# Nystrom attention into a sticky mixture of experts, one core: landmarks and C's row sums at other chunks, the first G in three pieces, and three smaller moves

## The chip, the cores and the metric

The kernel runs on one core of one Trainium2 chip. The metric is the device time of a run in microseconds (us), as the median of several runs. Engines are PE (matrix multiply), PEld (its weight loads), DVE (vector), ACT (scalar), POOL (GpSimd) and SP (the queue that issues most DMAs).

## The reference

```
# per batch b of 8; 8 heads, 576 tokens, 64 columns a head, 32 landmarks (means of 18 tokens)
A, Bm, C = sm(q, k_lm), sm(q_lm, k_lm), sm(q_lm, k)        # row softmaxes; C is 32 x 576
Z = Bm.T / (norm1(Bm) * norminf(Bm) + 1e-6)
for _ in range(6): Z = 2*Z - Z @ Bm @ Z
x = A @ Z @ C @ v                                          # 576 x 512 after joining the heads
logits = x @ w_gate;  local = sigmoid(x @ w_local)
# token s takes the expert of the token before it, unless s == 0 or local < 0.5: then argmax(logits)
p = softmax(logits)[e];  out[b, s] = p * (relu(x @ w1[e]) @ w2[e])     # 8 experts, 512 -> 1024 -> 512
```

## The kernel before

**What is computed where.** x is never formed. At, the transposed A (for all heads, 256 rows by 576 tokens), is split into a high and a low part (`ath`, `atl`); with W = Z C v, G = W w1[e] is formed once per batch in `w_w1` (L798: PE makes `pg` and `ph`; L804: ACT copies them rounded to `gh`; L807: DVE writes the rest, `gl`). `mm1` (L832) multiplies gh by ath, gh by atl and gl by ath into `ph`; ACT takes the relu (`h`, L839), DVE its low part (L844, and L847 for the last 64 tokens). The second product (L874, L883) multiplies h by `wh` and `wl`, the split of w2 (L819 on ACT, L821 on POOL), into `py` and `pg`. Each batch runs whole with the expert that most of its tokens chose; the other tokens go into 128 slots, which are done as a ninth, short pass.

**Order.** All of this is one stream written out by hand. An expert's pass over a batch is 16 chunks (`CH`), about 3.4 us each; `tick` advances a clock between chunks, and `at_time(t, fn)` queues a step that starts at chunk t and may `yield` a number of chunks before its next part. The attention of batch b is put in with `attention(b)`: each step has an offset in chunks to t0 = 16 (b - 1), from the table STEADY, or FIRST and SECOND for the batches 1 and 2. So the attention of a batch runs in pieces beside the expert passes of the one to three batches before it. In this text batch n is the stretch in which the expert's pass of batch n runs; batch 0 begins near 41 us, batch 1 near 106, and from there each takes 54.1 us; the slots' pass runs from about 466. A phase is a chunk within a batch. Every engine runs its instructions in program order and waits where one isn't ready.

**The steps that the change touches.** `load` brings q and k of a batch (two DMAs of 1152 KB on SP), `load_v` v. `landmarks` is called four times a batch (k, q, k, q): two adds on POOL (L200) into `t9`, of which there is one buffer, and a chunk later a reduce on DVE (L202), then ACT's scale (L210, L212). `c_sums` (L312 to L314) makes the reciprocal row sums of C, used by L299 in `c_v`. `gates` and `fresh` (L459 to L481) make the gate logits' maximum and the flag d (L478) that PE transposes at L490; `newton_start` (L358, L359) makes `et` for PE's L367. `own_rest` (L526 to L538) ends with a chain on a tile `psum`. `load_w1` and `load_w2` (L783, L812) bring the experts' weights as `raw`. `store` ends a block of 128 tokens; the last, half block adds two parts on POOL (L912) after ACT has read it (L909, L910). `others` finds the slots in batch 7: it sets tables with POOL memsets (L920, L921, L938) that a DVE scan reads (L927). `slot_tokens` makes one-hot rows on DVE (L1013) and gathers with them on PE (L1017); from the result come indices by which POOL fetches rows (L1040).

Of the kernel before, what the change touches and what calls it, by code (L numbers as in the profile page):

```python
# [12 lines left out]
F32 = mybir.dt.float32  # L13
# [4 lines left out]
ALU = mybir.AluOpType  # L18
# [42 lines left out]
def nystrom_attn_then_sticky_moe(ctx, tc, qT, kT, v, wg, w12, out):  # L61
    nc = tc.nc
# [70 lines left out]
    sm = ctx.enter_context(tc.tile_pool(name="sm", bufs=2))  # L133
# [24 lines left out]
    def at_time(t, fn, *args):  # L158
        heapq.heappush(events, (t, next(serial), fn, args))
# [12 lines left out]
    def at_once(parts):  # L172
        for _ in parts:
            pass
# [115 lines left out]
        nc.scalar.copy(out=st["ect"][0:rows, k0:k0 + nb, :], in_=pt[0:rows, 0:nb, :])  # L290

    def c_v(st):
        rs = c_sums(st)
        pv = one.tile([P, 2, D])
        for g in range(2):
            c_v_rows(st, pv, g, range(NBLK))
        yield 0.25
        st["u"] = sm.tile([P, 2, D], F32, name="u")
        nc.vector.tensor_tensor(out=st["u"], in0=pv, in1=rs.unsqueeze(2).broadcast_to([P, 2, D]), op=ALU.mult)  # L299
# [8 lines left out]
                                 st["v"][0:rows, k, D * h:D * h + D], start=(k == 0), stop=(k == NBLK - 1))  # L308

    def c_sums(st):  # L310
        rs = sm.tile([P, 2], F32, name="rsc")
        nc.vector.reduce_sum(out=rs, in_=st["sc"], axis=AX.X)  # L312
        nc.vector.tensor_scalar_add(rs, rs, 1e-9)
        nc.vector.reciprocal(out=rs, in_=rs)  # L314
        return rs
# [226 lines left out]
    def keep_busy(n):  # L542

        pz = one.tile([P, 512]).rearrange("p (a b) -> p a b", b=P)
        for _ in range(n):
            nc.tensor.matmul(pz, identb, ones.unsqueeze(1).broadcast_to([P, 4, P]), start=True, stop=True)

    def startup(st, nx):
# [77 lines left out]
        rs = sm.tile([P, 2], F32, name="rsb")  # L626
# [33 lines left out]
        rsc = c_sums(st)  # L660
# [15 lines left out]
        full = st["full"] = at.tile([P, 2, S], F32, name="at")  # L676
# [69 lines left out]
        own(0, st)  # L746

        e = st["e"] = expert_of(regs[0:1, 0:1])
        st["w1", 0] = load_w1(e, 0, 2)
        get_w2(0, 0)  # L750
        get_w2(0, 1)
        st["w1", 1] = load_w1(e, 1)
# [4 lines left out]
        lk0(2)  # L757
        c0 = scores_c(nx, 0)
        next(c0)
        keep_busy(5)  # L760
        lq2(4)
        rest = own_rest(0, st)
        next(rest)
        next(c0)
        nc.vector.tensor_tensor(out=al, in0=full, in1=ah.bitcast(F32), op=ALU.subtract)
        lk2(2)
        g0 = w_w1(st, 0, 0, 2)
        at_once(c0)
        next(g0)
        at_once(g0)  # L770
        at_once(rest)
        at_time(0.3, lk2, 2)

    behind = []

# [1 line left out]
        return nc.values_load(reg, engines=[ET.SP], min_val=0, max_val=E - 1,  # L777
                              skip_runtime_bounds_check_because="an expert")

    def load_w1(e, hf, nf=4):  # L780
        t = fw.tile([P, 4, 512], F32, name="raw1", bufs=2)
        for f in range(0, 4, nf):
            nc.sync.dma_start(out=t[:, f:f + nf], in_=w12[bass.ds(e, 1), 4 * hf + f:4 * hf + f + nf, :, 0:512].rearrange(  # L783
                "a f p x -> p (a f) x"))
        return t
# [111 lines left out]
    def store(b, st, k, yp):  # L897
        t0 = b * S + k * P
        if k < 4:
            ys = fk.tile([P, DM], F32, name="ys", bufs=2)  # L900
            nc.scalar.mul(out=ys, in_=yp, mul=st["pw"][:, k:k + 1])  # L901
            yield 0.5
            nc.sync.dma_start(out=out[t0:t0 + P, :], in_=ys)
        else:
            p = st["pw"][0:64, k:k + 1]
            yield 1.25
            ys = fk.tile([P, DM], F32, name="ys", bufs=2)
            yl = fk.tile([P, DM], F32, name="yl", bufs=1)
            nc.scalar.mul(out=ys[0:64], in_=yp[64:128], mul=p)  # L909
            nc.scalar.mul(out=yl[0:64], in_=yp[0:64], mul=p)  # L910
            yield 0.5
            nc.gpsimd.tensor_tensor(out=ys[0:64], in0=ys[0:64], in1=yl[0:64], op=ALU.add)  # L912
            yield 1
            nc.sync.dma_start(out=out[t0:t0 + 64, :], in_=ys[0:64])


    def others():

        segs = xp.tile([P, E * B, NBLK], F32, name="segs")
        nc.gpsimd.memset(segs, 1.0)  # L920
        nc.gpsimd.memset(segs[:, :, 0:1], 0.0)  # L921
        ohf = oh.rearrange("p e c -> p (e c)")
        pt, pp = [one.tile([P, 512])[:, 0:E * NCOL] for _ in range(2)]
        nc.tensor.matmul(pt, ones, ohf, start=True, stop=True)
# [9 lines left out]
        nc.vector.tensor_single_scalar(ti, ti, 7, op=ALU.arith_shift_right)  # L934
        cnt = xp.tile([P, E * B], F32, name="cnt")
        nc.vector.tensor_copy(out=cnt, in_=ti)
        one64 = xp.tile([P, E * B], F32, name="one64")
        nc.gpsimd.memset(one64, 1.0)  # L938
        end = xp.tile([P, E * B], F32, name="end")
        nc.vector.tensor_tensor_scan(out=end, data0=one64, data1=cnt, initial=0.0, op0=ALU.mult, op1=ALU.add)  # L940
        base = xp.tile([P, E * B], F32, name="base")
# [27 lines left out]
        nc.vector.reduce_sum(out=any_, in_=oh.rearrange("p e c -> p c e"), axis=AX.X)  # L969
        nc.vector.tensor_add(slot, slot, any_)  # L970
        nc.vector.tensor_mul(slot, slot, any_)
        now = xp.tile([P, 1], F32, name="now")
        nc.gpsimd.memset(now, 0.0)

        yield 0.75
        tabp = xp.tile([P, NCOL, 7], BF16, name="tabp")
# [5 lines left out]
        yield 0.75  # L982
        nc.vector.tensor_tensor(out=pr, in0=pr, in1=tabp[:, :, 5], op=ALU.subtract)
        nc.vector.tensor_copy(out=tabp[:, :, 6], in_=pr)
        xs.update(slot=slot, lo=lo, base=base, end=end, now=now, tabp=tabp)

    def slot_tokens(st):

# [22 lines left out]
        for c0 in range(0, NCOL, 8):  # L1011
            row = xp.tile([P, 8, P], BF16, name="row")
            nc.vector.tensor_tensor(out=row, in0=iota128.unsqueeze(1).broadcast_to([P, 8, P]),  # L1013
                                    in1=xs["lo"][:, c0:c0 + 8].unsqueeze(2).broadcast_to([P, 8, P]), op=ALU.is_equal)
            yield 1
            for c in range(8):
                nc.tensor.matmul(pi, row[:, c, :], rhs[:, c0 + c, :], start=(c0 + c == 0), stop=(c0 + c == NCOL - 1))  # L1017
        yield 0.75
# [78 lines left out]
    def cast_w2(b, f):  # L1097
# [84 lines left out]
    def slots_end():
        sts[B]["e"] = slot_weights(sts[B])
# [59 lines left out]
```

## Time and profile before

| what | value |
|---|---|
| median of the runs | 495.53 us (495.44 to 496.33) |
| the profiled execution's own time | 493.74 us |
| its span | 491.9 us |
| PE busy | 461.4 us, 94% of the span |
| DVE, ACT, POOL busy | 326.4, 211.2, 186.9 us |
| mean granted TensorE clock over the span | 0.981 of full speed |

The span is what the trace shows from the first instruction to the last; 1.84 us of the execution's own time lie around it. All durations in this text come from this one execution, which was 1.79 us below the median.

### The profile page before, as it was taken

Reading aid. Unit: us, or ns where it says so; the run is one execution under the profiler, and the core shown is the slowest. Engines: PE = TensorE matmul, PEld = TensorE weight load, DVE = VectorE, ACT = ScalarE, POOL = GpSimd, SP = SyncE. Lnnn points to the kernel's source line nnn. Section 1 sums busy time; section 2 is a strip of 40 time slices with the busy share of each in tenths; the row PEclk is TensorE's granted clock in tenths of the full one; section 3 lists DMA queues with packets and bytes.
Section 4 is the critical chain, followed back from the end, with each engine's and each line's share of the span. In section 5 each row is a group of like instructions: output and inputs, shape, how many; then the busy total and the mean of one; then the engine's idle time right before and its main releaser. Section 6 shows DMA issues by size and latency. Waiting matters only on the chain.

```text
span 491.9 us, 12153 instructions
## 1 busy us (share of the span) xinstructions
PE 461.4 (94%) x4722; PEld 342.2 (70%) x4722; DVE 326.4 (66%) x961; ACT 211.2 (43%) x538; POOL 186.9 (38%) x198
## 2 busy tenths in 40 slices
PE   6758999999999999999999999999999999899994
PEld 2424677667786778777786778677877877578873
DVE  7978787967859663876668664976456544975230
ACT  2425443545353543555253634454255414441551
POOL 6212261436324640456135620555015601441662
PEclk9858999999999999999999999999999999999999
DMA  8538836357526760839044941752063306432450
GB/s 304 195 144 286 322 126 192 121 197 245 184 90 243 228 229 1 306 113 340 33 173 161 284 173 43 268 177 109 1 237 141 125 0 237 157 127 102 121 159 20
DMA packets 38620, 82.58 MB, mean 168 GB/s; under 512 B 3179, under 2 KB 4459, under 8 KB 37792
## 3 DMA queue, kind: packets, MB, share of 16 engines
q1 hardware_dynamic: 37072, 76.71, 45.4%
q0 software_dynamic: 1488, 5.07, 2.7%
q8 instruction: 38, 0.62, 0.5%
q14 instruction: 22, 0.18, 0.1%
HBM read 66.34 MB, written 15.47 MB: 166 GB/s over the span
## 4 chain that ended last, share of the span: by engine, by line
PE 66%; DVE 23%; issue 3%; ACT 3%; DMA 2%; POOL 2%; SPq 0%; POOLq 0%; ACTq 0%; DVEq 0%
PE py L874 27%; PE ph L832 16%; PE pg L883 5%; PE one L260 3%; PE one L306 2%; PE one L367 2%; DVE gl L807 2%; DVE h L844 2%; PE one L287 2%; PE ph L798 2%; DVE psum L533 2%; DMA k_t<-kT 1%; DVE sa L411 1%; DVE sq L202 1%; DVE sk L202 1%
## 5 line engine op out<-in xcount | busy, mean ns | idle before, releaser
L874 PE MATMUL py<-wh,h 128*128 128x512 f32 x528 | 171.8, 407 | 0.1
L839 ACT ACTIVATE h<-ph 128x256 fp32r<-128x256 f32 (+2 forms) x136 | 54.5, 400 | 177.0 <-PE ph L832 159.8
L821 POOL TENSOR_TENSOR wl<-raw,wh 128x512 fp32r<-128x512 f32 x72 | 92.3, 1291 | 91.8 <-ACT wh L819 90.4
L874 PEld LDWEIGHTS py<-wh,h 128*128 128x128 f32 x528 | 89.5, 188 | 31.4 <-issue 20.2
L844 DVE SCALAR_TENSOR_TENSOR h<-ph,h 128x256 fp32r<-128x256 f32 (+1 forms) x136 | 54.9, 407 | 66.6 <-ACT h L839 64.5
L832 PE MATMUL ph<-ath,gh 128*128 128x320 f32 (+1 forms) x256 | 77.7, 304 | 6.9 <-DVE gl L807 3.5
L874 PE MATMUL py<-wl,h 128*128 128x512 f32 x264 | 83.4, 395 | 0.0
L832 PE MATMUL ph<-ath,gl 128*128 128x320 f32 (+1 forms) x256 | 75.8, 296 | 0.6 <-DVE gl L807 0.6
L832 PE MATMUL ph<-atl,gh 128*128 128x320 f32 (+1 forms) x256 | 75.5, 295 | 0.0
L832 PEld LDWEIGHTS ph<-ath,gh 128*128 128x128 f32 x256 | 48.2, 188 | 19.1 <-issue 5.7
L874 PEld LDWEIGHTS py<-wl,h 128*128 128x128 f32 x264 | 49.2, 188 | 10.8
L832 PEld LDWEIGHTS ph<-atl,gh 128*128 128x128 f32 x256 | 48.3, 189 | 4.2
L832 PEld LDWEIGHTS ph<-ath,gl 128*128 128x128 f32 x256 | 48.2, 188 | 1.2 <-DVE gl L807 1.0
L200 POOL TENSOR_TENSOR t<-q_t 128x288 f32<-128x288 f32 x20 | 14.5, 748 | 87.4 <-DVE sk L202 87.4
L819 ACT CAST wh<-raw 128x512 fp32r<-128x512 f32 x72 | 44.2, 618 | 0.0
L912 POOL TENSOR_TENSOR ys<-ys,yl 64x512 f32<-64x512 f32 x8 | 10.3, 1289 | 44.6 <-ACT yl L910 44.6
L901 ACT ACTIVATE ys<-py,pall 128x512 f32<-128x512 f32 x32 | 20.3, 686 | 6.4 <-PE py L874 6.4
L431 POOL TENSOR_TENSOR sa<-sa,rsa 128x1152 f32<-128x1152 f32 x7 | 14.9, 2132 | 18.9 <-PE one L383 14.3
L883 PE MATMUL pg<-wh,h 128*128 128x512 f32 x56 | 21.9, 392 | 0.0
L883 PE MATMUL pg<-wl,h 128*128 128x512 f32 x56 | 21.9, 392 | 0.0
L807 DVE TENSOR_TENSOR gl<-pg,gh 128x512 fp32r<-128x512 f32 (+1 forms) x19 | 12.4, 652 | 11.8 <-ACT gh L804 11.8
L419 POOL TENSOR_TENSOR sa<-sa,mxa 128x1152 f32<-128x1152 f32 x7 | 14.9, 2132 | 11.4 <-DVE mxa L417 10.7
(321 smaller groups left out, 746.1 us busy)
## 6 DMA issues: line engine op xcount, KB each, us to landing
raw<-w SPq DMA_DIRECT2D x72, 256.0 KB, 4.9
raw<-w SPq DMA_DIRECT2D x17, 1024.0 KB, 7.1
v_t<-v SPq DMA_DIRECT2D x8, 1024.0 KB, 6.3
out<-ys SPq DMA_DIRECT2D x32, 256.0 KB, 2.5
q_t<-qT SPq DMA_DIRECT2D x6, 1152.0 KB, 6.8
k_t<-kT SPq DMA_DIRECT2D x6, 1152.0 KB, 10.3
ad<-sa POOLq DMA_DIRECT2D x8, 576.0 KB, 6.3
q_t<-qT SPq DMA_DIRECT2D x4, 576.0 KB, 7.8
```

What stands on the lines that cost most here:

```text
L260: nc.tensor.matmul(pc[hf][32 * c:32 * c + 32, 0:n], st["ql"][r, h // 2, :], st["k"][r, h // 2, 288 * hf:288 * hf + n], start=True, stop=True)
L419: nc.gpsimd.tensor_tensor(out=sa, in0=sa, in1=mx.unsqueeze(2).broadcast_to([P, 2 * NJ, M]), op=ALU.subtract)
L431: nc.gpsimd.tensor_tensor(out=sa, in0=sa, in1=rs.unsqueeze(2).broadcast_to([P, 2 * NJ, M]), op=ALU.mult)
L807: nc.vector.tensor_tensor(out=gl[:, g, x], in0=ps[g], in1=gh[:, g, x].bitcast(F32), op=ALU.subtract)
L819: nc.scalar.copy(out=wh, in_=raw)
L821: nc.gpsimd.tensor_tensor(out=wl, in0=raw, in1=wh.bitcast(F32), op=ALU.subtract)
L832: mm = nc.tensor.matmul(hp, w[:, g, c], x[:, g, s0:s0 + n], start=(i == 0), stop=(i == 5))
L839: nc.scalar.activation(out=h[:, 0:e], in_=hp[:, 0:e], func=AF.Relu)
L844: nc.vector.scalar_tensor_tensor(out=h[:, 384:384 + m], in0=hp[:, 0:m], scalar=0.0, in1=h[:, 0:m].bitcast(F32), op0=ALU.max, op1=ALU.subtract)
L874: nc.tensor.matmul(yps[k], h[:, part + i * P:part + i * P + P], w, start=(f == 0 and part == 0 and w is wh), stop=(f == NC2 - 1 and part = ...
L883: nc.tensor.matmul(yps[4], hs[ff][1], w, start=(ff == 0 and w is w2[ff][0]), stop=(ff == NC2 - 1 and w is w2[ff][1]))
L901: nc.scalar.mul(out=ys, in_=yp, mul=st["pw"][:, k:k + 1])
```

## The change

`load` and the four `landmarks` of the batches 4 to 7 start four chunks earlier (STEADY); batch 3 keeps its old offsets in a table of its own (THIRD). `c_sums` is called half a chunk after the first `c_transpose` instead of at the head of `c_v`. In `startup` the w1 of batch 0 comes in pieces of 1, 1 and 2 blocks of 128 columns, G is made in the same three pieces, two of the matmuls that only keep PE busy go, and the order of the steps around changes; `own_rest` of batch 0 comes after the second piece; the first casts of w2 come later. The half block's ACT reads wait 2 chunks instead of 1.25. The memsets of the slots' tables are issued in `slots_begin`, which runs in batch 6, instead of in `others`. In `slot_tokens` PE's gather comes 1.25 chunks behind the one-hot rows instead of 1.

```diff
-        rs = c_sums(st)                      # c_v
+        rs = st["rsc"]
...
-        st["w1", 0] = load_w1(e, 0, 2)       # startup
+        st["w1", 0] = load_w1(e, 0, (1, 1, 2))
...
         c0 = scores_c(nx, 0)
         next(c0)
-        keep_busy(5)
         lq2(4)
+        nc.vector.tensor_tensor(out=al, in0=full, in1=ah.bitcast(F32), op=ALU.subtract)
+        next(c0)
+        keep_busy(3)
+        g0 = w_w1(st, 0, 0, 1)
+        next(g0)
+        at_once(c0)
+        at_once(g0)
+        lk2(2)
         rest = own_rest(0, st)
         next(rest)
-        next(c0)
-        nc.vector.tensor_tensor(out=al, in0=full, in1=ah.bitcast(F32), op=ALU.subtract)
-        lk2(2)
-        g0 = w_w1(st, 0, 0, 2)
-        at_once(c0)
-        next(g0)
-        at_once(g0)
-        at_once(rest)
+        at_time(0.2, w_w1, st, 0, 1, 1)
         at_time(0.3, lk2, 2)
+        at_time(1.2, w_w1, st, 0, 2, 2)
+        at_time(1.3, at_once, rest)
...
-            yield 1.25                       # store, the half block
+            yield 2
...
-        segs = xp.tile([P, E * B, NBLK], F32, name="segs")      # others; now in slots_begin
-        nc.gpsimd.memset(segs, 1.0)
-        nc.gpsimd.memset(segs[:, :, 0:1], 0.0)
+        segs, one64 = xs["segs"], xs["one64"]
...
-            yield 1                          # slot_tokens, ahead of L1017
+            yield 1.25
...
-    STEADY = dict(load=-26, landmarks=(-22.75, -21.5, -20.25, -19), load_v=-14, scores_c=(-13.75, -11.75), norms=-10.75,
+    STEADY = dict(load=-30, landmarks=(-27, -25.75, -24.5, -23.25), load_v=-14, scores_c=(-13.75, -11.75), norms=-10.75,
...
+    THIRD = dict(STEADY, load=-26, landmarks=(-22.75, -21.5, -20.25, -19))
...
+        at_time(t0 + t["turn"][0] + 0.5, c_sums, st)            # attention
...
-        at_time(f + (0.25 if f else 1), cast_w2, 0, f)
-    at_time(0.25, lambda: w_w1(sts[0], 0, 2, 2))
+        at_time(f + (1.5 if f == 0 else 1.25 if f == 1 else 0.5), cast_w2, 0, f)
```

In the changed file the lines above L762 keep their numbers, and those of `w_w1`, `mm1`, `split_w2` and `store` stand two higher (L798 is L800, L807 is L809, L844 is L846, L821 is L823, L912 is L914). Three places show the order of the instructions.

DVE in batch 2, phases 5 to 7: the gate logits are transposed (L461), then come the gates' chain to d and the start of Newton's iteration (`et`). Before:

```order
L461 STREAM_TRANSPOSE lg<-one 64x32
L467 TENSOR_REDUCE mxl<-lg 128x5
L470 TENSOR_TENSOR eq<-lg,mxl 128x40
L472 TENSOR_SCALAR fr<-lg 128x5
L473 TENSOR_TENSOR eq<-eq,desc_81 128x40
L474 MEMSET fr 1x1
L476 TENSOR_REDUCE am<-eq 128x5
L478 TENSOR_TENSOR d_2757<-fr,am 128x5
```

and of the change:

```order
L461 STREAM_TRANSPOSE lg<-one 64x32
L202 TENSOR_REDUCE sk<-t_2685 128x64
L467 TENSOR_REDUCE mxl<-lg 128x5
L470 TENSOR_TENSOR eq<-lg,mxl 128x40
L472 TENSOR_SCALAR fr<-lg 128x5
L473 TENSOR_TENSOR eq<-eq,desc_81 128x40
L474 MEMSET fr 1x1
L476 TENSOR_REDUCE am<-eq 128x5
L478 TENSOR_TENSOR d_2775<-fr,am 128x5
```

The first landmark reduce of batch 5 now stands between the transposed logits and the chain; its other three follow behind L494. The same holds in the batches 1, 3 and 4.

DVE at the end of batch 2, ahead of the second half's `gl` (the transposed scores `sa`, L411, stand next to it). Before:

```order
L411 STREAM_TRANSPOSE sa<-one 128x288 x2
L202 TENSOR_REDUCE sk<-t_2987 128x64
L844 SCALAR_TENSOR_TENSOR h<-ph,h 128x256
L370 TENSOR_TENSOR et<-et,one 128x2x32
L202 TENSOR_REDUCE sq<-t_3044 128x64
L411 STREAM_TRANSPOSE sa<-one 128x288 x2
L807 TENSOR_TENSOR gl<-pg,gh 128x512
```

and of the change:

```order
L411 STREAM_TRANSPOSE sa<-one 128x288 x2
L846 SCALAR_TENSOR_TENSOR h<-ph,h 128x256
L370 TENSOR_TENSOR et<-et,one 128x2x32
L411 STREAM_TRANSPOSE sa<-one 128x288 x2
L809 TENSOR_TENSOR gl<-pg,gh 128x512
```

Two reduces are gone from the rows ahead of gl.

DVE at the start of batch 0 (`psum` is the chain of `own_rest`, `hx` the low part for the last 64 tokens), from the second gl of the first piece on. This is the change; before, the chain stood between the first gl pair and the first h:

```order
L809 TENSOR_TENSOR gl<-pg,gh 128x128
L809 TENSOR_TENSOR gl<-ph,gh 128x128
L846 SCALAR_TENSOR_TENSOR h<-ph,h 128x256
L849 SCALAR_TENSOR_TENSOR hx<-ph,hx 128x64
L532 TENSOR_REDUCE psum<-pe 128x5
L533 TENSOR_SCALAR psum<-psum 128x5
L534 RECIPROCAL psum<-psum 128x5
L535 TENSOR_TENSOR pe<-pe,ohb 128x40
L536 TENSOR_REDUCE psum<-pe 128x5
L538 TENSOR_TENSOR pall<-psum 128x5
L809 TENSOR_TENSOR gl<-pg,gh 128x256
L809 TENSOR_TENSOR gl<-ph,gh 128x256
```

The chain moved behind the second piece's gl and the second h, and stands now ahead of the third piece's gl.

## Rows read from the trace of the kernel before

In rows of a timeline the columns are start us, length us, engine, line, operation, output <- input, partitions x elements and type, count; a bracket at the end is the idle time of the engine just before and what ended it.

**Rows 1.** The page's busy times of each engine (share of the span, instructions), and the first line of the waits of PE: line, what it waited for, us in total, times, longest.

```profile
PE 461.4 (94%) x4722; PEld 342.2 (70%) x4722; DVE 326.4 (66%) x961; ACT 211.2 (43%) x538; POOL 186.9 (38%) x198
...
PE ph L832 <- DVE gl L807: 4.2, 7, 0.7
```

**Rows 2.** PE's timeline at the ends of the batches 1, 2 and 4: the first mm1 of the second half of the next G.

```profile
157.13 0.36 PE L832 MATMUL ph<-ath,gh 128*128 128x256 f32 x1 [0.62 <-DVE gl L807]
...
211.22 0.35 PE L832 MATMUL ph<-ath,gh 128*128 128x256 f32 x1 [0.64 <-DVE gl L807]
...
319.41 0.35 PE L832 MATMUL ph<-ath,gh 128*128 128x256 f32 x1 [0.61 <-DVE gl L807]
```

**Rows 3.** The timelines of POOL, ACT and DVE at the end of batch 2, just ahead of that mm1.

```profile
206.91 1.45 POOL L200 TENSOR_TENSOR t<-q_t 128x288 f32<-128x288 f32 x2 [3.97 <-DVE sk L202]
...
208.44 0.59 ACT L804 CAST gh<-ph 128x512 fp32r<-128x512 f32 x1
...
208.39 0.75 DVE L202 TENSOR_REDUCE sq<-t 128x64 f32<-128x576 f32 x1 [0.92 <-POOL t L200]
209.82 0.65 DVE L807 TENSOR_TENSOR gl<-pg,gh 128x512 fp32r<-128x512 f32 x1
210.40 0.68 DVE L807 TENSOR_TENSOR gl<-ph,gh 128x512 fp32r<-128x512 f32 x1
```

**Rows 4.** The timelines of POOL, DVE and PE in batch 3, phases 6 to 8.

```profile
235.81 1.45 POOL L200 TENSOR_TENSOR t<-k_t 128x288 f32<-128x288 f32 x2 [3.79 <-DMA k_t<-kT]
...
236.50 0.20 DVE L467 TENSOR_REDUCE mxl<-lg 128x5 f32<-128x40 f32 x1
236.73 0.59 DVE L470 TENSOR_TENSOR eq<-lg,mxl 128x40 f32<-128x40 f32 x1
237.82 0.17 DVE L478 TENSOR_TENSOR d<-fr,am 128x5 bf16<-128x5 f32 x1
238.87 0.23 DVE L359 TENSOR_TENSOR et<-et,id 128x64 f32<-128x64 f32 x1
...
240.29 0.50 PE L490 MATMUL one<-identb,d 128*1 128x128 bf16 x5
240.72 0.43 PE L367 MATMUL one<-et 32*32 32x64 f32 x16
```

**Rows 5.** The timelines of POOL, DVE and PE in batch 1, the same steps.

```profile
129.71 1.29 POOL L821 TENSOR_TENSOR wl<-raw,wh 128x512 fp32r<-128x512 f32 x1 [2.52 <-ACT wh L819]
131.59 1.42 POOL L200 TENSOR_TENSOR t<-k_t 128x288 f32<-128x288 f32 x2 [0.59 <-DMA k_t<-kT]
...
129.80 1.22 DVE L478 TENSOR_TENSOR d<-fr,am 128x5 bf16<-128x5 f32 x1
131.76 0.64 DVE L359 TENSOR_TENSOR et<-et,id 128x64 f32<-128x64 f32 x1
...
131.29 0.50 PE L490 MATMUL one<-identb,d 128*1 128x128 bf16 x5
132.55 0.42 PE L367 MATMUL one<-et 32*32 32x64 f32 x16 [0.75 <-DVE et L359]
```

**Rows 6.** The DMA view of 216 to 240 us (batch 3): what was moved in it, and of the issues: operation, count, KB each, us from issue to landing.

```profile
DMA packets 2292, 5.62 MB, mean 234 GB/s; under 512 B 176, under 2 KB 304, under 8 KB 2160
...
k_t<-kT SPq DMA_DIRECT2D x1, 1152.0 KB, 11.0
```

**Rows 7.** ACT's timeline in batch 3: the cast of the last w2 block, and the next instruction.

```profile
230.05 0.61 ACT L819 CAST wh<-raw 128x512 fp32r<-128x512 f32 x1
232.14 0.29 ACT L271 ACTIVATE bm<-one,nm 128x32 f32<-128x32 f32 x1 [1.48 <-DVE nm L269]
```

**Rows 8.** The timelines of DVE and PE at the start of batch 0.

```profile
42.02 0.18 DVE L532 TENSOR_REDUCE psum<-pe 128x5 f32<-128x40 f32 x1
42.98 0.17 DVE L538 TENSOR_TENSOR pall<-psum 128x5 f32<-128x5 f32 x1
44.70 0.41 DVE L807 TENSOR_TENSOR gl<-ph,gh 128x256 fp32r<-128x256 f32 x1
46.02 0.21 DVE L847 SCALAR_TENSOR_TENSOR hx<-ph,hx 128x64 fp32r<-128x64 f32 x1
...
42.60 0.40 PE L798 MATMUL ph<-raw,wt 64*32 64x256 f32 x1
43.94 0.38 PE L832 MATMUL ph<-ath,gh 128*128 128x320 f32 x1 [0.68 <-DVE hx L847]
44.99 1.23 PE L260 MATMUL py<-k_t,ql 64*32 64x288 f32 x16
```

**Rows 9.** The timelines of POOL, DVE and PE in batch 7, where the slots are found.

```profile
413.89 1.29 POOL L912 TENSOR_TENSOR ys<-ys,yl 64x512 f32<-64x512 f32 x1 [21.34 <-ACT yl L910]
...
415.79 0.82 DVE L927 TENSOR_TENSOR_SCAN inc<-segs,one 128x320 f32<-128x320 f32 x1 [4.21 <-POOL segs L921]
...
416.99 0.61 PE L798 MATMUL ph<-raw,wt 64*32 64x512 f32 x1 [0.96 <-DVE h L844]
419.88 0.39 PE L832 MATMUL ph<-ath,gh 128*128 128x256 f32 x1 [1.04 <-DVE h L844]
422.94 0.36 PE L832 MATMUL ph<-ath,gh 128*128 128x256 f32 x1 [0.69 <-DVE gl L807]
```

**Rows 10.** PE's timeline in batch 7: the first gather of one-hot rows in `slot_tokens`.

```profile
439.55 0.36 PE L1017 MATMUL one<-rhs,row 128*128 128x7 bf16 x8 [0.91 <-DVE row L1013]
```

More of the change, by code (lines that the diff above doesn't have):

```diff
@@ L310, in c_sums @@
     def c_sums(st):
-        rs = sm.tile([P, 2], F32, name="rsc")
+        rs = st["rsc"] = sm.tile([P, 2], F32, name="rsc")
         nc.vector.reduce_sum(out=rs, in_=st["sc"], axis=AX.X)
@@ L778, in expert_of, with load_w1 @@
                               skip_runtime_bounds_check_because="an expert")
-    def load_w1(e, hf, nf=4):
+    def load_w1(e, hf, parts=(4,)):
         t = fw.tile([P, 4, 512], F32, name="raw1", bufs=2)
-        for f in range(0, 4, nf):
+        for f, nf in zip(itertools.accumulate((0,) + parts), parts):
             nc.sync.dma_start(out=t[:, f:f + nf], in_=w12[bass.ds(e, 1), 4 * hf + f:4 * hf + f + nf, :, 0:512].rearrange(
@@ L936, in others @@
         nc.vector.tensor_copy(out=cnt, in_=ti)
-        one64 = xp.tile([P, E * B], F32, name="one64")
-        nc.gpsimd.memset(one64, 1.0)
         end = xp.tile([P, E * B], F32, name="end")
@@ L971, in others @@
         nc.vector.tensor_mul(slot, slot, any_)
-        now = xp.tile([P, 1], F32, name="now")
-        nc.gpsimd.memset(now, 0.0)
         yield 0.75
@@ L984, in others @@
         nc.vector.tensor_copy(out=tabp[:, :, 6], in_=pr)
-        xs.update(slot=slot, lo=lo, base=base, end=end, now=now, tabp=tabp)
+        xs.update(slot=slot, lo=lo, base=base, end=end, tabp=tabp)
     def slot_tokens(st):
@@ L1116, in attention @@
         st, t0 = sts[b], (b - 1) * CH
-        t = {1: FIRST, 2: SECOND}.get(b, STEADY)
+        t = {1: FIRST, 2: SECOND, 3: THIRD}.get(b, STEADY)
         def steps(name, fn, *args):
@@ L1180, in slots_begin @@
         xp = ctx.enter_context(tc.tile_pool(name="xp", bufs=1, side="right"))
+        segs = xs["segs"] = xp.tile([P, E * B, NBLK], F32, name="segs")
+        nc.gpsimd.memset(segs, 1.0)
+        nc.gpsimd.memset(segs[:, :, 0:1], 0.0)
+        xs["one64"] = xp.tile([P, E * B], F32, name="one64")
+        nc.gpsimd.memset(xs["one64"], 1.0)
+        xs["now"] = xp.tile([P, 1], F32, name="now")
+        nc.gpsimd.memset(xs["now"], 0.0)
     def slots_end():
```

## The prediction

> **What bounds the kernel.** I read the busy times first: PE works 94% of the span and DVE 66% [rows 1]. So a microsecond counts only if PE stands still for it, and I went through the list of PE's waits. Its largest entry that repeats is the mm1 at L832 that waits for DVE's `gl`: 4.2 us in 7 waits [rows 1]. In PE's timeline four of them stand at the ends of the batches 1 to 4, each 0.61 to 0.64 us [rows 2]: these are the batches in which the landmarks of the batches 4 to 7 run. Then I read the other engines' timelines around each place that the change touches, for which row is late and how much room it has.
>
> The terms go against this execution's own time, 493.74 us. It is 1.79 below the median, so I add the sum to 495.53. About 0.2% (1 us) is what a measurement of this kernel can tell from no change.
>
> **The landmarks leave the batch's end.** At the end of batch 2 ACT has finished gh at 209.03, but DVE still works through the landmark reduce (L202, 0.75), a transpose and the first gl, and the second gl ends at 211.08; PE stood 0.64 [rows 2, 3]. No row between the reduce and gl shows DVE idle, so everything behind it comes up to 0.75 earlier, more than the 0.64 that PE misses. The adds on POOL are paired with the reduce through the one buffer `t9` (POOL waited 3.97 for it [rows 3]), and go too. Four times 0.61 to 0.64: **-2.5 us**.
>
> **The landmarks arrive in phase 5 to 9.** What was removed comes back elsewhere: the first reduce now precedes the chain to d. In batch 3 the chain runs from L467 at 236.50 to L478's end at 237.99; PE wants d at 240.29, so it has 2.30 to spare. L359 ends at 239.10 and PE's L367 starts at 240.72: 1.62 [rows 4]. Some 0.15 of each is the way from DVE to PE, as L359's end at 132.40 and L367's start at 132.55 show [rows 5], so the room is about 2.15 and 1.47. What is added ahead of both: the reduce, 0.73; and what POOL does to the chain. As soon as the reduce frees `t9`, POOL starts the next two adds; in the rows it followed at once, and two adds take 1.45 [rows 3]. L470, a DVE operation on two tiles in SBUF, took 0.59 while such adds ran, against 0.17 to 0.23 of the small operations around it, and d's L478 took 1.22, to 131.02, while POOL's L821 ran from 129.71 to 131.00 [rows 4, 5]. So I take it that the chain waits for the first of the adds and again for the second: 0.95 in all, bounded by 0.35 (only the first, the remainder of one add) and 1.2. The old 0.39 at L470 falls away. Sum: 0.73 + 0.95 - 0.39 = 1.29.
>
> The Trainium skill (SBUF — State Buffer, section Who interferes with whom) says that of a DVE instruction with two SBUF inputs and a GpSimd instruction that reads SBUF the one that issues second blocks fully until the first is done, and that issue order decides. L478's row agrees: 1.22 long, ending 0.02 behind POOL. By the rule alone the adds cost between 0, where DVE's operation comes first, and 1.45 less what of the chain fits before them; the sum for one batch would be 0.3 to 1.6. It is the ground for two of the rivals below.
>
> Ahead of that stands the norms' chain, which before ran beside an idle POOL and in the new order meets L821 and the first pair of adds. I add 0.5 (0 to 1.4). So the chain is late by 1.8 (0.7 to 2.9), and with 1.47 of room PE stands 0.35 to 0.4 in each of the batches 2 to 4: **+1.2 us** (0 to +4). In batch 1 there is no room: PE already stood 0.75 at L367, since L478 and L359 were held by POOL [rows 5]. There the reduce counts nearly whole, and the holds are dealt anew: **+0.7 us** (-0.5 to +1.7).
>
> The loads: v, q and k now follow each other on SP, ahead of the last w2 block, whose cast ran at 230.05 with 1.48 of idle time behind it [rows 7]. Over that stretch the queues moved 5.62 MB at a mean of 234 GB/s [rows 6]. The three loads and the block are 3.8 MB; from v's issue near 218 that is 16 us at this mean, which is 234, 4 late; but the mean holds empty slices, and k alone landed in 11.0 us [rows 6] behind q and the other traffic. I take that the block lands near 231.5 and the cast is up to 1 late, inside its idle time; the 0 to 1.4 above covers it. The same skill (SBUF — State Buffer, A bandwidth-pool intuition that's wrong) gives about 358 GB/s between HBM and a core; as an estimate by that page the 3.8 MB take 10.6 us, to 228.6, and the cast is not late. No row here shows that rate over so long a stretch.
>
> **C's row sums.** Three small DVE operations leave the start of the next batch and run in phase 8. PE's list of waits has none on them, so I set 0.
>
> **The start.** Two busy matmuls fewer and a first piece of half the size let the first mm1 begin some 0.85 earlier, which I get by laying the new rows end to end with the old durations. But the order on DVE then costs: before, the psum chain (42.02 to 43.15, 1.13) held back L847, and PE stood 0.68 for it; the third and fourth blocks' gl was done at 45.11, before PE came to them at about 46.2 [rows 8]. After, the second block's G lies between, so that its mm1 ends at about 44.85, 0.2 earlier than before. From the mm1's end to L847's end DVE and ACT took 46.23 - 44.99 = 1.24 [rows 8]; then comes the psum chain, 1.13, then the third gl pair, twice 0.41: 3.2 after mm1's end. PE has only the third piece's G, 0.66 (42.60 to 43.26, where its wait begins), and L260, 1.23, to fill this: 1.9. gl is the last of the three products, which gives PE some 0.3 more, so it stands for about 1, and against the old order the third piece's G lies 0.66 in the way instead of in the old stall. Sum -0.2 + 0.66 + 1.0 = 1.5, of which I leave 0.5 to later slack: **+1.0 us** (-0.5, where the psum chain slips behind, to +2).
>
> **The slots' tables.** In batch 7 the half block's add on POOL (413.89 to 415.18) stood ahead of the memsets, and DVE's scan waited 4.21 us for these, to 415.79; the low part of h came behind it, and PE stood 0.96 at L798 [rows 9]. With the memsets done in batch 6 (POOL then idles for most of 21.34 us [rows 9]) the scan needs only its matmul and is over before h. The 0.96 goes. The other two waits here, 1.04 and 0.69, sit behind a row of DVE work that starts that much earlier, as PE does; I count 0.1 of them: **-1.1 us** (-0.9 to -1.3).
>
> **The gather** comes a quarter chunk later and has other PE work ahead of it: of the 0.91 [rows 10] half goes, **-0.4 us** (-0.8 to +0.5; the fetches of the slots start later by about a chunk). The **half block** read later shifts one store by a raw load: 0.
>
> Sum: -2.5 + 1.2 + 0.7 + 1.0 - 1.1 - 0.4 = **-1.1 us**, own time 492.6, median 494.4.
>
> **Rivals.** *The chain is held everywhere* (the other side): from 2.1 us of delay on, PE pays more than it gained. With the upper bounds, 1.3 in each of the batches 2 to 4 and 1.7 in batch 1, the sum is -2.5 + 3.9 + 1.7 + 1.0 - 1.5 = +2.6: 498.1. For it speaks that both kinds of holds are in the rows of batch 1; against it, 1.47 of room in batch 3. Chance 0.27. *DVE slips through*: the chain's operations come ahead of the adds or between them, the delay stays under 1.47, and batch 1 loses nothing: -2.5 + 1.0 - 1.5 = -3.0, 492.5. For it: before, L470 lost only 0.39. Chance 0.18. *The start gains*: ACT and DVE have more slack than I see, and it gives -0.5 instead of +1: -2.6, 492.9. Chance 0.12. *My sum*: 493.4 to 495.9, chance 0.43.
>
> Faster takes the two gaining rivals and 0.19 of my own: 0.49. Same: 0.22 of mine and 0.01 of the first rival. Slower: the rest, 0.28. The range of 8 in 10 leaves out both gaining rivals happening together (491.0) and the first with a start of +2: 491.8 to 498.2.
>
> **What would show it.** The gl waits at the four batch ends gone; small waits on d or `et` (L478, L359) in the batches 1 to 4, with L202 just ahead of L467 and L470 or L473 longer than 0.2; the psum chain ahead of the third gl near 46 us and a wait there; the scan near 412.4 and no wait of PE at 416. I am wrong if the `et` waits are near zero or well over 0.5 a batch, if the block's late landing moves the cast past 232.2, or if PE meets its first L874 no later than before.

## The result, and the profile after

The changed kernel took 500.53 us in the median of 20 runs, the kernel before 496.09 in 20 runs beside it; the ratio is 1.0081, with an interval of 1.0057 to 1.0105, so it is about 4 us slower. The forecast was 494.4 with a range to 498.2. The runs of the changed kernel lie far apart, from 495.94 to 503.35, those of before from 494.49 to 497.84. The profiled execution is the longest of them, 503.35 with a span of 501.3: its trace shows more than the median paid. The runs with a mean granted clock of 0.965 to 0.969 are those of 500.75 and longer; with 0.974 or more all lie below 499.1.

The page of the changed kernel, with the first lines of PE's waits (us in total, times, longest):

```profile
PE 464.7 (93%) x4736; PEld 345.8 (69%) x4736; DVE 321.5 (64%) x963; ACT 212.7 (42%) x540; POOL 186.9 (37%) x198
...
PE ph L834 <- DVE gl L809: 3.4, 4, 1.5
PE one L1042 <- DMA xa<-ad,gi: 2.7, 1, 2.7
PE one L490 <- DVE d L478: 2.5, 4, 1.0
PE one L367 <- DVE et L359: 2.4, 5, 0.6
```

PE is busy for 3.3 us more than before, though it runs hardly any more instructions: part of its work ran at half clock. The four gl waits at the batch ends [rows 2] are gone; what is left on that line are others. New is a wait of 2.7 for the rows that are fetched for the slots, and the waits on d (L478) and et (L359) in these lines are nine, where before had two, both on et.

The same instruction of PE in both traces tells where the span's 9.4 us arose. Start of an instruction before, after, and the lag:

| instruction | before | after | lag |
|---|---|---|---|
| d's transpose (L490) ahead of batch 0, ahead of the changed code | 30.06 | 30.71 | 0.65 |
| L490 in batch 0 | 83.98 | 87.52 | 3.54 |
| L490 in batch 5, after the moved landmarks | 348.52 | 352.71 | 4.19 |
| the ones' product (L513) of batch 6 | 408.24 | 412.44 | 4.20 |
| first gather (L1017, now L1013) | 439.55 | 443.25 | 3.70 |
| last instruction of PE ends | 485.34 | 494.76 | 9.42 |

The start made 2.9, the batches 1 to 4 net 0.65, the slots' tables -0.5, and the stretch from the first gather to the end 5.7. The first 0.65 are from code that is the same in both.

**The start.** Timelines of DVE and PE:

```profile
46.28 0.18 DVE L532 TENSOR_REDUCE psum<-pe 128x5 f32<-128x40 f32 x1
47.24 1.26 DVE L538 TENSOR_TENSOR pall<-psum 128x5 f32<-128x5 f32 x1
...
48.88 0.42 PE L834 MATMUL ph<-ath,gl 128*128 128x320 f32 x1 [1.54 <-DVE gl L809]
```

The psum chain (from 46.28) stands ahead of the third gl, as the prediction read from the order, and PE waits 1.54 at it. Its last operation, L538, took 1.26 instead of 0.17 [rows 8]. PE's busy time and granted clock (third column) in the stretches around:

```profile
48.00:50.00 2.00, 1.11 (x20) 1.00 0.16 45
50.00:53.00 3.00, 3.00 (x24) 0.51 1.04 393
```

Behind the wait the granted clock was 0.51 for 3 us, about half and so its lower level of 1.2 GHz, while PE was fully busy.

**Batch 3, phases 6 to 8.** Timelines of ACT, POOL, DVE and PE; they answer to [rows 4] and [rows 7]:

```profile
235.39 0.62 ACT L821 CAST wh<-raw 128x512 fp32r<-128x512 f32 x1 [2.05 <-DMA raw<-w]
...
236.08 1.30 POOL L823 TENSOR_TENSOR wl<-raw,wh 128x512 fp32r<-128x512 f32 x1 [3.51 <-ACT wh L821]
242.16 1.45 POOL L200 TENSOR_TENSOR t<-q_t 128x288 f32<-128x288 f32 x2 [3.38 <-DVE sk L202]
...
236.32 1.09 DVE L320 TENSOR_SCALAR rsb<-sb 128x2 f32<-128x2 f32 x1 [1.27 <-ACT bm L271]
241.38 0.70 DVE L202 TENSOR_REDUCE sk<-t 128x64 f32<-128x576 f32 x1
242.22 0.74 DVE L470 TENSOR_TENSOR eq<-lg,mxl 128x40 f32<-128x40 f32 x1
242.89 0.75 DVE L472 TENSOR_SCALAR fr<-lg 128x5 f32<-128x5 f32 x1
244.01 0.17 DVE L478 TENSOR_TENSOR d<-fr,am 128x5 bf16<-128x5 f32 x1
...
244.23 0.50 PE L490 MATMUL one<-identb,d 128*1 128x128 bf16 x5 [0.59 <-DVE d L478]
245.28 0.43 PE L367 MATMUL one<-et 32*32 32x64 f32 x16 [0.55 <-DVE et L359]
```

Read it from the top. ACT's cast of the last w2 block waits 2.05 for its DMA; before it ran with no wait [rows 7]. Behind it ACT makes `bm`, so DVE idles 1.27 ahead of L320, and L320 then lasts 1.09, until POOL's L823, which the late cast moved here, is over. So the chain comes late to L202. The reduce releases the adds at 242.16; L470 and L472 take 0.74 and 0.75 behind them, and d ends 0.05 before L490 starts. The Trainium skill (SBUF — State Buffer, Who interferes with whom) says that of a DVE instruction with two SBUF inputs and a GpSimd instruction that reads SBUF the one that issues second waits until the first is done; L470 agrees, ending at 242.96, near the end of the first of the two adds (an estimate: half of their 1.45, 242.89).

**The slots' tables, batch 7.** Timelines of POOL, DVE and PE:

```profile
423.72 3.79 POOL L823 TENSOR_TENSOR wl<-raw,wh 128x512 fp32r<-128x512 f32 x3 [6.86 <-DMA raw<-w]
...
425.09 1.21 DVE L952 TENSOR_SCALAR ri<-ri 128x40 int32<-128x40 int32 x1
426.33 1.22 DVE L955 CAST lo<-ri 128x40 f32<-128x40 int32 x1
427.56 0.41 DVE L846 SCALAR_TENSOR_TENSOR h<-ph,h 128x256 fp32r<-128x256 f32 x1
...
428.02 0.41 PE L834 MATMUL ph<-ath,gh 128*128 128x320 f32 x1 [1.87 <-DVE h L846]
```

The scan no longer waits, and the three waits of [rows 9] are gone. But DVE's rank chain now runs while POOL has its three L823 in a row: L952 takes 1.21 and L955 1.22, the low part of h comes behind them, and PE waits 1.87. From 429 to 432 us the granted clock was 0.50.

**The slots' rows.** Timelines of POOL and PE, then PE's stretches (us, busy, clock):

```profile
461.77 1.10 POOL L1036 DMA_INDIRECT xa<-ad,gi  x1 [17.44 <-DVE fx L1022]
471.00 1.00 POOL L1036 DMA_INDIRECT xa<-ad,gi  x1 [0.30 <-issue]
...
473.64 0.45 PE L1042 MATMUL one<-ident,xa 128*128 128x128 f32 x1 [2.72 <-DMA xa<-ad,gi]
475.39 0.55 PE L834 MATMUL ph<-ath,gh 128*128 128x256 f32 x1 [1.30 <-DVE gl L809]
```

```profile
474.00:480.00 6.00, 4.70 (x17) 0.50 0.49 153
```

The fetches run from 461.77 to 472.00, and the second transpose of their rows waits 2.72, gl another 1.30. From 474 to 480 us the clock was 0.50, with PE busy for 4.70 of the six.

### The profile page after: what moved, and what is told of

Read it like the earlier page. It is cut to its first block, busy times and chain, and to the rows that moved or that the text cites. A ratio compares the mean times of both kernels' runs of the same rounds, so it can differ in the third digit from the quotient of the medians.

```text
span 501.3 us, 12197 instructions
## 1 busy us (share of the span) xinstructions
PE 464.7 (93%) x4736; PEld 345.8 (69%) x4736; DVE 321.5 (64%) x963; ACT 212.7 (42%) x540; POOL 186.9 (37%) x198
## 4 chain that ended last, share of the span: by engine, by line
PE 63%; DVE 18%; DMA 9%; issue 3%; ACT 2%; SPq 2%; another core or an unknown queue 1%; POOL 1%; POOLq 0%; DVEq 0%; ACTq 0%
PE py L876 27%; PE ph L834 15%; DMA raw<-w 7%; PE pg L885 4%; PE one L367 3%; PE one L306 2%; PE one L407 2%; PE one L287 2%; PE one L260 2%; DMA k_t<-kT 2%; DVE h L846 1%; PE ph L800 1%; DVE gl L809 1%; PE pg L800 1%
## 5 line engine op out<-in xcount | busy, mean ns | idle before, releaser
L823 POOL TENSOR_TENSOR wl<-raw,wh 128x512 fp32r<-128x512 f32 x72 | 92.3, 1292 | 126.4 <-ACT wh L821 119.4
L846 DVE SCALAR_TENSOR_TENSOR h<-ph,h 128x256 fp32r<-128x256 f32 (+1 forms) x136 | 55.4, 408 | 68.5 <-ACT h L841 63.1
L876 PEld LDWEIGHTS py<-wl,h 128*128 128x128 f32 x264 | 50.3, 191 | 11.6
L821 ACT CAST wh<-raw 128x512 fp32r<-128x512 f32 x72 | 44.2, 618 | 7.0 <-DMA raw<-w 7.0
L914 POOL TENSOR_TENSOR ys<-ys,yl 64x512 f32<-64x512 f32 x8 | 10.3, 1284 | 68.9 <-ACT yl L912 68.9
L809 DVE TENSOR_TENSOR gl<-pg,gh 128x512 fp32r<-128x512 f32 (+2 forms) x20 | 12.7, 636 | 22.1 <-ACT gh L806 22.1
L806 ACT CAST gh<-pg 128x512 fp32r<-128x512 f32 (+2 forms) x20 | 10.9, 545 | 28.9 <-PE pg L800 12.8
```

The lines of the kernel that those rows point to most:

```text
L809: nc.vector.tensor_tensor(out=gl[:, g, x], in0=ps[g], in1=gh[:, g, x].bitcast(F32), op=ALU.subtract)
L821: nc.scalar.copy(out=wh, in_=raw)
L823: nc.gpsimd.tensor_tensor(out=wl, in0=raw, in1=wh.bitcast(F32), op=ALU.subtract)
L846: nc.vector.scalar_tensor_tensor(out=h[:, 384:384 + m], in0=hp[:, 0:m], scalar=0.0, in1=h[:, 0:m].bitcast(F32), op0=ALU.max, op1=ALU.subtract)
L876: nc.tensor.matmul(yps[k], h[:, part + i * P:part + i * P + P], w, start=(f == 0 and part == 0 and w is wh), stop=(f == NC2 - 1 and part = ...
```

## The experiments

Ratios are to the kernel before on the same chip. The medians of before differ between the chips and hours (493.97 to 496.20), so medians are compared only with the one beside them.

### Each part undone in the changed kernel

*u_gather* puts the gather's `yield` back to 1, *u_start* the start, *u_land* the offsets of load and landmarks, *u_tabs* the memsets.

```diff
-            yield 1.25          # u_gather: slot_tokens
+            yield 1
...
-    STEADY = dict(load=-30, landmarks=(-27, -25.75, -24.5, -23.25),      # u_land
+    STEADY = dict(load=-26, landmarks=(-22.75, -21.5, -20.25, -19),
```

> The changed kernel with only the gather's step put back from 1.25 chunks to 1. Theory A (the late fetch): the quarter chunk is paid five times over, the indices come about 4.5 us late against the batch, PE stands 2.7 us for the fetched rows and then runs at half clock for several us. With 1 the first fetch starts near 457.5, PE's wait for the fetched rows and the half-clock stretch at the slots' start are gone, and the time falls by 4 to 6 us, to 495 to 497. Theory B (the rival on record, the chain to d held by POOL in the batches 1 to 4 is the cost): the time falls by less than 1 us, since those waits stay.

> The changed kernel with only the start of batch 0 put back (w1 in two halves, the old order of the steps, the old times of the casts). Theory A (the psum chain ahead of the third gl, then half clock): the stretch up to 55 us is 2.5 to 3 us shorter, no half clock at 50 to 54, and the time falls by 2 to 3 us. Theory B (batches 1 to 4 are the cost): under 1 us.

> The changed kernel with only the old offsets of load and landmarks. Theory A: the four gl waits at the batch ends come back (2.5 us) and the waits on d and et in the batches 1 to 4 (about 3.1 us) go, so the time is the same within 1 us. Theory B: the time falls by 3 us or more.

> The changed kernel with only the memsets of the slots' tables put back into batch 7. Theory A (the move gains, as on record): the wait of DVE's scan for the memsets is back, and the time rises by about 1 us. A rival: what the move gains is given back by the one long wait of PE (1.9 us) and the half clock behind it at 428 to 432 us that the changed kernel shows, so the time is the same or falls by up to 1 us.

| run | median | ratio to before | interval |
|---|---|---|---|
| the change | 500.53 | 1.0081 | 1.0057 to 1.0105 |
| u_gather | 498.06 | 1.0048 | 1.0026 to 1.0069 |
| u_start | 500.41 | 1.0097 | 1.0064 to 1.0130 |
| u_land | 499.01 | 1.0066 | 1.0047 to 1.0086 |
| u_tabs | 499.98 | 1.0073 | 1.0043 to 1.0103 |

Undoing the gather gave the most, 0.3%, less than the 4 to 6 us expected, and its interval overlaps the change's; none of the four can be told from the change with certainty, since its own runs spread over 7 us. In u_gather's trace the wait for the fetched rows is gone, but another stands at the slots' first G (PE's timeline), where the trace of before has none:

```profile
466.73 0.61 PE L800 MATMUL ph<-raw,xwt 64*32 64x512 f32 x1 [1.85 <-DVE h L846]
```

The traces of land_late, land_2 and start_psum below have it too, 1.78 to 1.90 long. What makes h late there was not tried and stays open. For u_start the expectation of 2 to 3 us failed: its trace leads the changed kernel's by 2.75 us up to batch 1 and by 0.1 in batch 3, where the last w2 block was later still: ACT's cast waited 3.52 for it and PE 1.45 at L354, where the changed kernel has no wait of PE. So I turned to one part at a time on the kernel before, whose runs lie closer.

### Each part alone on the kernel before

> The kernel before with only the gather's quarter chunk. Theory A (late fetch): the first fetch starts 4 us later or more, PE stands for the fetched rows at the slots' start (about 2.7 us) and at the gl behind it, and the granted clock falls to half there: 2 to 5 us slower than before. Theory B (the waits on d and et in the batches are the cost): within 1 us of before.

> The kernel before with only the new offsets of load and landmarks (and batch 3's table). Theory A: four gl waits of 0.6 us go, waits on d and et of 0.9 to 1.5 us a batch come in the batches 1 to 4: 1 to 2 us slower. The rival on record (DVE slips through): 2 to 3 us faster.

> The kernel before with only the new start. Theory A: 2 to 3 us slower, with the wait of about 1.5 us at the third gl near 48 us and half clock behind it. A rival, since undoing the start in the changed kernel left its time the same: the lateness is absorbed by slack in the batches behind, and the time is within 0.5 us of before.

> The kernel before with only the slots' tables set in batch 6. Theory A: 0.5 to 1.5 us faster, with PE's waits at 416 to 423 us gone. The rival: DVE's rank chain, now earlier, meets POOL's run of three L821 and one wait of 1.8 us with half clock behind it takes the place of the three: the same within 0.5 us or up to 1 us slower.

| run | median | before | ratio | interval |
|---|---|---|---|---|
| o_gather | 497.59 | 494.34 | 1.0056 | 1.0043 to 1.0070 |
| o_land | 496.09 | 494.34 | 1.0036 | 1.0016 to 1.0055 |
| o_start | 495.75 | 494.34 | 1.0031 | 1.0018 to 1.0043 |
| o_tabs | 493.50 | 494.34 | 0.9987 | 0.9974 to 1.0001 |

The gather and the landmarks came out as theory A had it. The start is between its two expectations, and for the tables the middle is in theory A's range, but the interval includes no change. They add to 1.10% against the change's 0.81%, whose interval reaches to 1.05%. The quarter chunk of the gather is the dearest part. Timelines of POOL and PE before, the last fetch and the transposes of the fetched rows:

```profile
462.38 1.00 POOL L1040 DMA_INDIRECT xa<-ad,gi  x1 [0.30 <-issue]
...
464.78 0.44 PE L1046 MATMUL one<-ident,xa 128*128 128x128 f32 x2
```

These fetches took 2.4 us from issue to landing, so the last rows were there at 464.78, just as PE came to them: there was no room. Timelines of POOL and PE in o_gather, then PE's stretches:

```profile
458.73 1.10 POOL L1040 DMA_INDIRECT xa<-ad,gi  x1 [17.44 <-DVE fx L1026]
...
470.57 0.30 PE L1046 MATMUL one<-ident,xa 128*128 128x128 f32 x1 [2.68 <-DMA xa<-ad,gi]
```

```profile
471.00:475.00 4.00, 4.00 (x18) 0.58 0.70 204
```

The first fetch starts 5.6 us later than the 453.14 of the trace of before (0.55 of it is a lag from ahead of this place). The transposes moved too, to 467.61, but only by 2.8, and the second waits 2.68; the 4 us behind it have a mean clock of 0.58. In o_tabs PE's timeline of batch 7 answers to [rows 9]:

```profile
418.49 0.39 PE L832 MATMUL ph<-ath,gh 128*128 128x256 f32 x1 [0.46 <-DVE h L844]
...
421.30 0.36 PE L832 MATMUL ph<-ath,gh 128*128 128x256 f32 x1 [0.43 <-DVE gl L807]
...
426.33 0.61 PE L798 MATMUL ph<-raw,wt 64*32 64x512 f32 x1 [0.63 <-DVE h L844]
```

The 0.96 is gone, the 1.04 and 0.69 became 0.46 and 0.43, and a 0.63 stands at a later L798, which did not wait before: the waits are shorter, but DVE's chain still sets the pace.

### What in the gather costs: the wait or the clock

```diff
         for g in range(2):
+            if g == 1:
+                keep_busy(10)
             nc.tensor.transpose(out=px[:, g, :], in_=xa[:, g].rearrange("p c l -> p (c l)"), identity=ident)
```

> The kernel before with only the gather's quarter chunk, and ten matmuls of no use ahead of the second transpose of the fetched rows, which PE runs while it waits for them. Theory A (the wait and half clock behind it both cost): the wait falls from 2.7 to about 0.5 us, the clock stays full behind it, and of the 2.8 us that the quarter chunk costs 1 to 1.5 come back. Rival (only the wait for the rows counts): the same as the gather's quarter chunk alone, within 0.5 us.

The ratio to before is 0.9992 (0.9978 to 1.0006): the cost of the quarter chunk is gone. PE's timeline and stretches:

```profile
467.04 2.32 PE L546 MATMUL one<-ones,identb 128*128 128x512 bf16 x10
469.82 0.30 PE L1048 MATMUL one<-ident,xa 128*128 128x128 f32 x1 [0.46 <-DMA xa<-ad,gi]
```

```profile
471.00:475.00 4.00, 4.00 (x33) 1.00 0.87 262
```

The ten matmuls of no use take the place of the wait, and the clock stays full. From the first gather to PE's end took 45.79 us before, 49.29 in o_gather and 47.62 here, so in the traces the half clock is 1.7 of 3.5 and the wait 1.8. The times say more, 3.2 us between the two ratios, and leave nothing for the wait. The trace of before is an execution 1.79 us below its median, which may be the difference; no run shows it.

### The landmarks: the reduce, or the loads

*land_late* and *land_2* have the start and the gather of before, and the tables, row sums and half block of the change. *load_only* and *l28_only* are the kernel before with nothing else changed. *change_l28* is the whole change.

```diff
-    STEADY = dict(load=-30, landmarks=(-27, -25.75, -24.5, -23.25),      # the change
+    STEADY = dict(load=-30, landmarks=(-26, -24.75, -23.5, -22.25),      # land_late
+    STEADY = dict(load=-28, landmarks=(-25.75, -24.5, -23.25, -22),      # land_2, l28_only, change_l28
+    STEADY = dict(load=-30, landmarks=(-22.75, -21.5, -20.25, -19),      # load_only
```

> Start and gather as before; tables, C's row sums and half block as in the change; load at -30 as in the change, but each landmark one chunk later (-26 to -22.25), which puts the first reduce (L202) behind et (L359) on DVE. Theory A (the reduce and the adds that it releases, ahead of d and et, are what the new landmarks cost): the waits at L490 and L367 in the batches 2 to 4 are gone, the gl waits stay gone, and with the tables' gain it is 2 to 3.5 us faster than before. The rival (the loads at -30 are the cost, by the late w2 block and the norms' chain): waits at L354, L490 and L367 stay and it is within 1 us of before.

> As land_late, but load at -28 and the landmarks at -25.75 to -22: the loads leave SP two chunks later, and the first reduce stands behind L494. Theory A: like land_late, 2 to 3.5 us faster than before. Rival (loads): better than land_late by 1 us or more.

> The kernel before with only load at -30; the landmarks keep their old offsets. Theory A (the three loads ahead of the last w2 block are the cost of the move): the block lands 3 us late, ACT's cast waits for it and holds bm behind it, the gl waits stay, and PE waits at L354, L490 or L367 in the batches 1 to 4: 2 to 4 us slower than before. Rival (the first reduce ahead of d is the cost, the loads are hidden): within 0.5 us of before.

> The whole change, but load at -28 and the landmarks at -25.75 to -22. Theory A (parts add up: start 1.4, gather 2.8, tables -0.8, landmarks now -4 to -5): 0 to 2 us faster than before, 4 to 6 us faster than the change. Rival (the start's late batches eat the gain): 2 us slower than before or more.

> The kernel before with only load at -28 and the landmarks at -25.75 to -22. Theory A: 3.5 to 5 us faster than before (the best kernel so far, which also has the tables in batch 6, was 5.5). Rival (the tables' move is worth more together with it): 2 to 3 us faster.

| run | median | before | ratio | interval |
|---|---|---|---|---|
| land_late | 495.32 | 496.20 | 0.9992 | 0.9973 to 1.0011 |
| land_2 | 490.72 | 496.20 | 0.9887 | 0.9867 to 0.9907 |
| load_only | 496.37 | 493.97 | 1.0057 | 1.0031 to 1.0083 |
| l28_only | 489.43 | 493.97 | 0.9912 | 0.9880 to 0.9943 |
| change_l28 | 492.77 | 493.97 | 0.9984 | 0.9964 to 1.0003 |

The times went against my theory and with its rival, the loads. With the reduce out of d's way land_late gained almost nothing; the loads alone, with the landmarks where they were, cost 0.57%, 2.8 us. Batch 3 in o_land, load_only and land_late (timelines of ACT, DVE and PE):

```profile
233.86 0.62 ACT L819 CAST wh<-raw 128x512 fp32r<-128x512 f32 x1 [3.51 <-DMA raw<-w]
...
234.79 1.06 DVE L320 TENSOR_SCALAR rsb<-sb 128x2 f32<-128x2 f32 x1 [2.73 <-ACT bm L271]
...
237.03 0.33 PE L354 MATMUL one<-bt 32*32 32x32 f32 x16 [1.43 <-DVE s L333]
```

```profile
236.64 0.62 ACT L819 CAST wh<-raw 128x512 fp32r<-128x512 f32 x1 [3.54 <-DMA raw<-w]
...
239.82 0.33 PE L354 MATMUL one<-bt 32*32 32x32 f32 x16 [1.44 <-DVE s L333]
```

```profile
233.30 0.62 ACT L819 CAST wh<-raw 128x512 fp32r<-128x512 f32 x1 [3.54 <-DMA raw<-w]
...
236.47 0.33 PE L354 MATMUL one<-bt 32*32 32x32 f32 x16 [1.42 <-DVE s L333]
```

In all three the cast waits 3.5 us for the last w2 block, and PE then waits 1.4 at L354, for a sum (L333) that hangs on ACT's bm. In load_only it waits 0.99 there in batch 2 as well, and its trace loses 2.75 from L490 in batch 0 to the ones' product of batch 6, as much as the times say.

The reduce costs too. The waits at L490 and L367 in the batches 2 to 4 stand in the traces of the change and of o_land, and are gone in load_only and land_late, where no reduce stands ahead of d. Taking the tables' 0.13% off land_late, the times leave about 0.3% between it and o_land for the reduce, with intervals of 0.2% on each: the smaller part. The row sums and the half block, which land_late has and o_land hasn't, are in this difference. land_late's trace is its fastest run, 2.4 us below its median, so where the median lost can't be read in it.

In land_2 the loads stand behind that block on SP (timelines of ACT, POOL and DVE):

```profile
227.88 0.61 ACT L819 CAST wh<-raw 128x512 fp32r<-128x512 f32 x1
...
234.00 1.47 POOL L200 TENSOR_TENSOR t<-k_t 128x288 f32<-128x288 f32 x2 [4.15 <-DMA k_t<-kT]
...
238.68 0.45 DVE L492 TENSOR_SCALAR old<-one 1x576 bf16<-1x576 bf16 x1 [1.69 <-PE one L490]
```

The cast runs without a wait, POOL's first adds follow when k has landed, and DVE again has 1.69 to spare ahead of L492. From L490 in batch 3 to L490 in batch 4 took 54.09 us before and 52.95 here: 1.14 a batch, more than the 0.64 of the listed wait; what the other 0.5 are stays open. The whole change with these offsets can't be told from before (0.16% faster, and the interval includes no change); by the two ratios it is 4.8 us faster than with its own. land_2 and l28_only beat both kernels, and their intervals overlap.

The loads hardly moved with -28. SP's timelines of before and of l28_only in batch 3:

```profile
223.84 0.87 SPq L180 DMA_DIRECT2D q_t<-qT  x1
```

```profile
222.64 0.46 SPq L180 DMA_DIRECT2D q_t<-qT  x1
```

In both q leaves SP behind the last w2 block and 16.5 us ahead of L490 (240.29 and 239.14); in the batches 2 and 4 it is the same. So in the batches 2 to 4 what l28_only moves is the landmarks, and these gain; load_only moves the loads, and these lose.

### The start: the psum chain

```diff
-        at_time(1.3, at_once, rest)
+        at_time(2.3, at_once, rest)     # on o_start
```

> The kernel before with only the new start, but own_rest's psum chain one chunk later, behind the third gl on DVE. Theory A (the chain ahead of gl makes the start slow): the wait of 1.55 us at 48.5 us falls to about 0.3, and of the 1.4 us that the new start costs alone at least 1 comes back, to within 0.5 us of before. Rival (the third piece's G in PE's way and the first pieces' round trips are the cost): at most 0.5 us comes back.

The ratio is 1.0017 (1.0002 to 1.0032), against 1.0031 (1.0018 to 1.0043) with the chain ahead of gl: half came back, by intervals that overlap, so neither expectation is met. The traces agree: up to L490 of batch 1, less the lag at L490 ahead of batch 0, o_start is 0.92 behind before and start_psum 0.41. PE's timeline of o_start, then DVE's and PE's of start_psum:

```profile
48.47 0.42 PE L834 MATMUL ph<-ath,gl 128*128 128x320 f32 x1 [1.55 <-DVE gl L809]
56.85 0.41 PE L834 MATMUL ph<-ath,gl 128*128 128x320 f32 x1 [0.60 <-DVE gl L809]
```

```profile
47.58 0.18 DVE L532 TENSOR_REDUCE psum<-pe 128x5 f32<-128x40 f32 x1
...
55.49 0.41 PE L834 MATMUL ph<-ath,gl 128*128 128x320 f32 x1 [1.84 <-DVE gl L809]
```

The wait of 1.55 is gone, and the next one, at the second G's gl, grew from 0.60 to 1.84. The chain ahead of gl cost what was read, and most of it moved on to the next late row.

## Why the prediction was wrong

- **Which step failed most: the gather.** The sum had -0.4 for it, with the late fetches as an aside worth at most +0.5. Alone it cost 0.56%, about 2.8 us, a miss of 3.2; the landmarks with their loads missed by 2.4, the start and the tables by 0.5 each. Of the single parts only it and the landmarks (-0.6 net in the sum, 0.36% slower alone) had the wrong sign. The quarter chunk stands in a loop of five; the last indices come 1.25 chunks later, and the fetches in a chain of eight behind: 5.0 us, where the text had about a chunk. The rows of the fetches were there to be set against the transposes of what they bring, and this room, which was nothing, was not worked out.
- **The loads** were the second. The text worked out 16 us from v's issue to the last w2 block's landing, from the mean of 234 GB/s [rows 6], and then took 231.5 by an argument about empty slices. In o_land v was issued at 217.75 and the cast began at 233.86: 16.1 us. The cast, which the text took to be up to 1 late, was 3.8 late (3.1 without the 0.73 by which this trace lay behind in batch 2), past the 232.2 that the prediction had named as a sign of being wrong, and the 1.4 that were to cover it were too little. The landing by the 358 GB/s of the Trainium skill (SBUF — State Buffer, A bandwidth-pool intuition that's wrong), 228.6, was further off. That the three loads stand ahead of the block was seen in the order; that ACT holds `bm` behind the cast was in [rows 7], as 1.48 of idle time, and was spent as if it were all there for free.
- **The reduce ahead of d** was right in kind: L470 and L472 are held as read, and PE waits 0.93 to 1.15 in each of the batches 2 to 4 at L490 and L367, against 0.35 to 0.4 in the sum, and 1.52 in batch 1, where the sum had 0.75 + 0.7. The size was off: with the room of 2.15, the 0.59 at L490 in batch 3 make d 2.7 late, where the sum had 1.8 and 2.9 as the bound. The sum left the loads out of this lateness but for the 1.4; load_only and land_late show what they do alone, 1.4 at L354.
- **The gl waits** went, as said, -2.5 in the rows; with the loads out of the way a batch gained 1.14 rather than 0.64 in land_2's trace.
- **The start** was right in mechanism and near in size: +1.0 in the sum, 0.31% or 1.5 us alone, with a wait of 1.5 at the place that was named. Missed: L538 took 1.26, and the half clock behind the wait in some executions.
- **The tables**: -1.1 in the sum, 0.13% or 0.6 us alone, and the interval includes no change. The wait of 1.87 that takes the place of the three in the changed kernel was not foreseen; o_tabs alone doesn't have it.
- The rival on record (the chain held everywhere, 498.1) had the right sign, and its waits came at L490 and L367, but it named neither the gather nor the loads. C's row sums and the later half block were not tried alone.

## What to carry to other kernels

A step in a loop that gets a fraction more is paid once for each turn, and what follows it must be checked against the last moment at which its result is needed. Before loads are moved ahead of a small one on the same queue, divide the bytes up to its end by the mean rate of that stretch (here 234 GB/s gave 16 us, and 16.1 were measured), not by the best one, and look at what stands behind its first reader on that engine. Moving the landmarks' work paid here only once the loads stayed behind the small one: 0.9 to 1.1%.

## What the runs showed of the hardware

A wait of PE doesn't cost its length alone. After waits of 1.5 to 2.7 us the granted clock fell to its lower level for 3 to 6 us (0.51 at 50 to 53 us, 0.50 at 429 to 432 and at 474 to 480 in the changed kernel), but not each time: behind the same wait of 1.55 at 48.5 us o_start's trace has a clock of 1.00, where the changed kernel's had 0.51. The stretch in o_start (us, busy, clock):

```profile
50.00:53.00 3.00, 2.86 (x13) 1.00 0.95 384
```

The changed kernel, with three such waits, has runs spread over 7 us, against 3 before, and its runs with the lowest mean clock are the longest; that this chance makes the spread is argued, not shown. Ten useless matmuls in such a wait brought back 0.6%.
